# One matmul in place of two: global rows set beside the last batch's tokens in a fused sparse-attention and MLP kernel

## The chip, the cores and the metric

The kernel runs on one core of a Trainium2 chip. The metric is the device time of one execution in microseconds (us), as the median of several runs; a lower value is better. The kernel before took 382.2 us (median of 3 runs, 379.91 to 382.34). TensorE is called PE here, its weight loads PEld, VectorE DVE, ScalarE ACT, GpSimd POOL and SyncE SP, as in the profile.

## The reference: what is computed

Eight batches of 576 tokens go through eight heads of attention (head size 64). A token sees the tokens at most 32 away, and 8 global tokens, which every token sees and which see all tokens. The result, 4608 rows of 512 values, goes through a layer with 2048 inner values: `h = x @ w_in`, `g = h + sin(alpha*h)^2 / alpha`, `g @ w_out`.

```python
mask = np.abs(pos[:, None] - pos[None, :]) <= 32
mask = mask | is_global[:, None] | is_global[None, :]
scores = np.where(mask, scores, -1e9)
attn = softmax(scores)                  # rows
x = (attn @ v) as rows of 4608 x 512
h = x @ w_in                            # 512 -> 2048
s = np.sin(alpha * h)
out = (h + s * s / (alpha + 1e-9)) @ w_out
```

## The kernel before

The kernel works batch by batch. For batch b, `attention(b)` (L712) makes the normalised rows `xT`, and `gemm1(b)` (L947) makes the first product, the sine and its square, and writes the sum `g` to `H2`. `gemm2(b)` (L1028) is the second product; it is a generator, and `fill(n)` (L1069) issues its next n matmuls of 512 columns (L1033) wherever PE would have little else to do. The instructions are written in the order in which each engine takes them; each engine works through its own list in that order and waits on semaphores.

`attention` goes over four pairs of heads `hp`. For each it makes scores in three groups (L736), the exponential on ACT (L744), the mask on DVE (L747), the two products with the values and with ones (L778), an inverse of the sums on ACT (L804, L807), and on DVE two small sums over the pieces of the global rows (`sums`, L788) and the product with the inverse (`normalise`, L810). A token's row is normalised there. The 8 global rows of a batch are collected in `GS`, and after the last pair L859 takes the inverse and L860 writes them to column b of `XG`, which at the end holds 64 columns: 8 global rows times 8 batches. Besides, `beside(at)` adds small work at each pair, such as copies of the next batch's queries and keys (L347) and the squares of x (`square_x`, L892).

`gemm1` goes over 16 groups `nt` of 128 inner values. A group takes 4 steps `c` of the 512 inputs, times two halves `e` of 288 tokens: 8 matmuls (L972). Three buffers in PSUM take turns (`zn`, `zr`, `zd`), so that group nt+3 writes the buffer of group nt. The first two groups begin with steps c = 0 to 2, which need the first three pairs of heads only. After a group ACT takes the sine (L1009), ACT or DVE squares it (L1013 on ACT for nt 1, 3, 5, 8, 10, 12, 14; otherwise L1015 on DVE), and DVE makes the sum (L1020). Five matmuls of `gemm2` come after group 2, one after each of the groups 3 to 13.

In `gemm1` of the last batch (b = 7) the 64 global columns are worked too, 32 beside each half:

```python
nc.tensor.matmul(out=h[e][:, 0:HALF], lhsT=lhsT, rhs=xT[:, c, e, :], ...)         # L972
if more:
    nc.tensor.matmul(out=h[e][:, HALF:W], lhsT=lhsT,                              # L977
                     rhs=xg[:, c, e * NE : (e + 1) * NE], ...)
```

So each of 128 matmuls of 288 columns is followed by one of 32 columns with the same weights, loaded again. The sine and the square are taken over 2 x 320 columns at once, and a second, small L1020 writes the global part to `HG`.

Beside the result the kernel bounds the argument of the sine, by norms: `square_x` squares the rows and adds them up to 288 columns, `token_norms` (L903) multiplies those by ones on PE (L905) and compares on DVE (L907), and `global_norms` (L912) does the same for `XG` by a square (L916), four matmuls of 64 columns (L918) and a comparison (L920). Four of the eight `token_norms` and `global_norms` stand at the end: after the last `gemm1` come `square_x(7)`, 32 matmuls of `gemm2`, these norms, 16 more matmuls, the verdict (`judge`, L925, with one matmul, L939), the rest of `gemm2`, and the 64 global rows (`gemm2_globals`, L1051), which are written by an indirect DMA (L1061).

Of the kernel before, what the change touches and what calls it, by code (L numbers as in the profile page):

```python
# [10 lines left out]
ALU = mybir.AluOpType  # L11
AF = mybir.ActivationFunctionType
DT = mybir.dt
# [3 lines left out]
P = 128  # L17
KW = 96
NG = 8
KT = 48  # L20
# [227 lines left out]
def kernel(  # L248
# [11 lines left out]
    nc = tc.nc  # L260
# [24 lines left out]
    trp = mctx.enter_context(tc.tile_pool(name="trp", bufs=1))  # L285
    pairp = mctx.enter_context(tc.tile_pool(name="pairp", bufs=2))
    normp = mctx.enter_context(tc.tile_pool(name="normp", bufs=2))
    xpool = mctx.enter_context(tc.tile_pool(name="xpool", bufs=2))
    spool = mctx.enter_context(tc.tile_pool(name="spool", bufs=3))
    osbp = mctx.enter_context(tc.tile_pool(name="osbp", bufs=3))  # L290
    srp = mctx.enter_context(tc.tile_pool(name="srp", bufs=4))
# [19 lines left out]
    SQ = main.tile([P, CT * S], DT.bfloat16, name="SQ")  # L311
# [397 lines left out]
    xTs = {}  # L709


    def attention(b, beside):  # L712


        kx, qx, VXb = KX[b % 2], QX[b % 2], VX[b % 2]
        xT = xpool.tile([P, CT, 2, HALF], DT.bfloat16, name="xT")
        xTs[b] = xT
        GS = normp.tile([P, 2, NHP, 2, 4], DT.float32, name="GS")
        if b:
# [88 lines left out]

        def normalise(hp):
            nc.vector.tensor_tensor(  # L810
                out=xT[:, hp].rearrange("p e (k m c) -> p (e k) m c", k=2, c=KT), in0=body(hp, 0),
                in1=Rs[hp][:], op=ALU.mult,
            )

        start, per_scores = (START, PER_SCORES) if b != 1 else (0, LATE)
        def idle(hp):
            if (b == 0 and hp > 1) or (b == 1 and hp < 2):
                warm(zo[0], 1)

        fill(start)  # L820
        beside(-1)
        for hp in range(NHP):
            Es[hp] = pairp.tile([P, NT12, WCOL], DT.bfloat16, name="E")
            for g in range(2):
                scores(hp, g)
                fill(per_scores[hp][g])
                idle(hp)
            if b == 0 and hp:
                products(hp - 1, range(3), (1,))
            elif hp:  # L830
                products(hp - 1, (0, 1))
            scores(hp, 2)
# [12 lines left out]
        last = NHP - 1  # L845
# [13 lines left out]
        nc.vector.reciprocal(out=RG[:], in_=GS[:, 1])  # L859
        nc.vector.tensor_tensor(  # L860
            out=XG[:, :, :, b].rearrange("p h (c x) -> p h x c", x=2), in0=GS[:, 0], in1=RG[:], op=ALU.mult
        )
        beside(NHP)
        after.release()

# [25 lines left out]

    def square_x(b, part):  # L892

        xf = xTs[b][:].rearrange("p c e s -> p (c e s)")
        if part == 0:
            nc.vector.tensor_tensor(out=SQ[:], in0=xf, in1=xf, op=ALU.mult)
            return
        for n in (2 * S, S):
            nc.vector.tensor_tensor(out=SQ[:, 0:n], in0=SQ[:, 0:n], in1=SQ[:, n : 2 * n], op=ALU.add)
        SR[b] = srp.tile([P, HALF], DT.bfloat16, name="SR")  # L900
        nc.vector.tensor_tensor(out=SR[b][:], in0=SQ[:, 0:HALF], in1=SQ[:, HALF:S], op=ALU.add)

    def token_norms(b, pn):  # L903

        nc.tensor.matmul(out=pn[:, 0:HALF], lhsT=ones[:], rhs=SR.pop(b)[:], start=True, stop=True)  # L905
        low = normp.tile([P, HALF], DT.bfloat16, name="low")
        nc.vector.tensor_scalar(  # L907
            out=low[:], in0=pn[:, 0:HALF], scalar1=limit[:, 0:1], scalar2=0.0, op0=ALU.is_le,
            op1=ALU.add, accum_out=XC[:, b : b + 1],
        )  # L910

    def global_norms(pn):  # L912

        sg = normp.tile([P, CT, NG * B], DT.bfloat16, name="sg")
        xf = XG[:].rearrange("p c j b -> p c (j b)")
        nc.vector.tensor_tensor(out=sg[:], in0=xf, in1=xf, op=ALU.mult)  # L916
        for c in range(CT):
            nc.tensor.matmul(out=pn[:, 0 : NG * B], lhsT=ones[:], rhs=sg[:, c, :], start=c == 0, stop=c == CT - 1)  # L918
        low = normp.tile([P, NG * B], DT.bfloat16, name="lowg")
        nc.vector.tensor_scalar(  # L920
            out=low[:], in0=pn[:, 0 : NG * B], scalar1=limit[:, 0:1], scalar2=0.0, op0=ALU.is_le,
            op1=ALU.add, accum_out=XCG[:, 0:1],
        )

    def judge(pv):  # L925

        ok = [normp.tile([P, 1], DT.float32, name=f"ok{i}") for i in range(4)]
        for i, (src, lim, op) in enumerate(
            ((EA, LIM_SUM, ALU.is_le), (RA, LIM_REC, ALU.is_le), (XC, HALF - 0.5, ALU.is_ge),
             (XCG, NG * B - 0.5, ALU.is_ge))  # L930
        ):
# [15 lines left out]
    def gemm1(b):  # L947
# [1 line left out]

        xT = xTs[b]  # L950
        r0 = (b % 2) * S
        NE = NG * B // 2
        more = b == B - 1
        W = HALF + (NE if more else 0)
        xg = XG[:].rearrange("p c j b -> p c (j b)")
        hr = tc.alloc_tile_pool(name="hr", bufs=1, space=PSUM)
        hs = {}

# [2 lines left out]
        def chunks(nt, cs):  # L961
            if nt not in hs:
                if order[nt] == "o":
                    hs[nt] = [(slice(e, e + 1), zo[e][:, None, :]) for e in range(2)]
                else:
                    h = {"n": zn, "d": zd}.get(order[nt]) or hr.tile([P, 2, 512], DT.float32, name="zr")
                    hs[nt] = [(slice(0, 2), h[:])]
            h = [ap[:, i] for es, ap in hs[nt] for i in range(es.stop - es.start)]
            for c in cs:
                for e in range(2):  # L970
                    lhsT = w_in[:, c, nt * P : (nt + 1) * P]
                    nc.tensor.matmul(  # L972
                        out=h[e][:, 0:HALF], lhsT=lhsT, rhs=xT[:, c, e, :],
                        start=(c == 0), stop=(c == CT - 1), skip_group_check=True,
                    )
                    if more:
                        nc.tensor.matmul(  # L977
                            out=h[e][:, HALF:W], lhsT=lhsT, rhs=xg[:, c, e * NE : (e + 1) * NE],
                            start=False, stop=(c == CT - 1), skip_group_check=True,
                        )  # L980

        on_act = (ON_ACT_FIRST, ON_ACT_SECOND, ON_ACT)[min(b, 2)]
        for nt in range(NT):
# [29 lines left out]
                nc.scalar.activation(out=s2[:, :, 0:W], in_=sb[:, :, 0:W], func=AF.Square)  # L1013
            else:
                nc.vector.tensor_tensor(out=s2[:, :, 0:W], in0=sb[:, :, 0:W], in1=sb[:, :, 0:W], op=ALU.mult)  # L1015
            for dst, lo, hi in (
                (H2[:, nt, r0 : r0 + S], 0, HALF), (HG[:, nt, :], HALF, HALF + NE)
            )[: 1 + more]:
                for es, h in hs[nt]:
                    nc.vector.scalar_tensor_tensor(  # L1020
                        out=dst.rearrange("p (e c) -> p e c", e=2)[:, es],
                        in0=s2[:, es, lo:hi], scalar=recipT[:, nt : nt + 1], in1=h[:, :, lo:hi],
                        op0=ALU.mult, op1=ALU.add,
                    )
        hr.release()


# [168 lines left out]
```

## Time and profile before

| what | value |
|---|---|
| median of 3 runs | 382.2 us (379.91 to 382.34) |
| the profiled execution: its own time | 381.18 us |
| the profiled execution: span from first to last instruction | 379.5 us |
| granted TensorE clock, mean | 0.991 |
| busy: PE, DVE, ACT, POOL | 342.2, 288.4, 294.3, 133.8 us |
| matmuls; weight loads | 3172; 3172 |

Times are us from the start of the span. A row of the timeline has a start, a duration, the engine, the line, the operation, what it writes and reads with shapes, how often, and in brackets the idle time of the engine before it and what ended that. A group row ends in the busy time, the mean duration in ns, and the idle time before. Matmuls overlap: one takes longer from its start to its end than the distance to the next one's start, so the price of a matmul is read from the distance between starts. The same holds, less strongly, for DVE and ACT.

### The profile page before, as it was taken

What the parts mean: (1) busy time and instruction counts of PE and PEld (TensorE: products, weight loads), DVE (VectorE), ACT (ScalarE), POOL (GpSimd) and SP (SyncE); (2) the same over time, 40 slices, a digit from 0 to 9 for tenths busy, and PEclk for the clock granted to TensorE, in tenths of its full rate; (3) what the DMA queues carried; (4) which work ended last, traced back from release to release, by engine and by line L of the source; (5) the groups of instructions that cost most, each with busy time, mean ns of one, the idle gap of its engine ahead of it and who ended that gap; (6) DMA issues with size and microseconds to landing.
All of it is one profiled execution on the core that took longest, in us unless ns stands there. A gap on an engine that the chain in (4) does not pass through costs nothing. (4 is left out here: it accounts for less than half of the span.)

```text
span 379.5 us, 8635 instructions
## 1 busy us (share of the span) xinstructions
PE 342.2 (90%) x3172; PEld 233.3 (61%) x3172; DVE 288.4 (76%) x614; ACT 294.3 (78%) x566; POOL 133.8 (35%) x204
## 2 busy tenths in 40 slices
PE   2679869997998899999989999999999998999893
PEld 2567646764565666676656766666676666776341
DVE  6777897589889887988888888888788876589400
ACT  7789897898889788788878887889888888675111
POOL 7993695559477101840086006720000000000001
PEclk9999999999999999999999999999999999999998
DMA  6999999999999863789069923727111011100221
GB/s 119 119 161 186 155 153 174 147 173 179 182 181 119 137 114 74 91 99 216 28 81 94 204 62 45 75 40 155 42 44 29 0 41 46 29 3 28 57 85 48
DMA packets 103579, 38.08 MB, mean 100 GB/s; under 512 B 94138, under 2 KB 98250, under 8 KB 103082
## 3 DMA queue, kind: packets, MB, share of 16 engines
q0 software_dynamic: 56640, 18.56, 42.4%
q1 hardware_dynamic: 46890, 18.89, 25.1%
q8 instruction: 27, 0.44, 0.5%
q14 instruction: 22, 0.18, 0.1%
HBM read 37.15 MB, written 17.83 MB: 145 GB/s over the span
## 5 line engine op out<-in xcount | busy, mean ns | idle before, releaser
L1033 PE MATMUL zo<-w_out,H 128*128 128x512 bf16 x576 | 153.2, 378 | 0.0
L972 PEld LDWEIGHTS <-w_in 128*128 128x128 bf16 x1024 | 99.2, 97 | 48.4 <-issue 14.8
L390 POOL DMA_DIRECT2D VX<-in_v_dram x128 | 83.7, 663 | 105.7 <-PE zd L778 87.4
L1033 PEld LDWEIGHTS <-H 128*128 128x128 bf16 x576 | 52.0, 97 | 37.3
L744 ACT ACTIVATE E<-ring 128x480 bf16<-128x480 f32 x96 | 54.3, 568 | 24.5 <-PE ring L736 24.0
L972 PE MATMUL zn<-xT,w_in 128*128 128x288 bf16 x376 | 56.2, 285 | 4.7 <-DVE H L1020 2.0
L747 DVE TENSOR_TENSOR E<-E,MASK 128x480 bf16<-128x480 bf16 x96 | 36.6, 411 | 16.2 <-ACT E L744 15.0
L972 PE MATMUL zr<-xT,w_in 128*128 128x288 bf16 x312 | 46.7, 285 | 1.0 <-DVE H L1020 0.6
L972 PE MATMUL zd<-xT,w_in 128*128 128x288 bf16 x312 | 45.4, 285 | 1.6 <-DVE H L1020 1.5
L1020 DVE SCALAR_TENSOR_TENSOR H<-s,recipT,zn 128x576 bf16<-128x576 bf16 x47 | 38.2, 813 | 9.9 <-ACT s L1013 5.5
L1061 POOL DMA_INDIRECT out_dram<-osb,grow x1 | 1.0, 1007 | 125.8 <-SPq L1164 125.8
L1009 ACT ACTIVATE sb<-zn,alphaT 128x576 bf16<-128x576 f32 (+1 forms) x47 | 34.8, 741 | 12.6 <-PE zn L972 9.2
L1013 ACT ACTIVATE s<-sb 128x576 bf16<-128x576 bf16 (+1 forms) x62 | 42.7, 689 | 2.0
L736 PE MATMUL ring<-QX,KX 128*128 128x120 bf16 x384 | 38.3, 226 | 5.6 <-ACT E L744 2.7
L736 PEld LDWEIGHTS <-KX 128*128 128x128 bf16 x384 | 29.1, 102 | 21.7 <-issue 7.6
L1015 DVE TENSOR_TENSOR s<-sb 128x576 bf16<-128x576 bf16 (+1 forms) x66 | 31.4, 475 | 7.7 <-ACT sb L1009 7.4
L1020 DVE SCALAR_TENSOR_TENSOR H<-s,recipT,zd 128x576 bf16<-128x576 bf16 x39 | 31.7, 813 | 6.6 <-ACT s L1013 4.8
L1039 ACT COPY osb<-zo 128x512 f32<-128x512 f32 x36 | 20.8, 578 | 19.7 <-PE zo L1033 19.7
L1020 DVE SCALAR_TENSOR_TENSOR H<-s,recipT,zr 128x576 bf16<-128x576 bf16 x39 | 31.7, 813 | 4.6 <-ACT s L1013 2.5
L1009 ACT ACTIVATE sb<-zd,alphaT 128x576 bf16<-128x576 f32 (+1 forms) x39 | 28.9, 741 | 7.9 <-PE zd L972 5.3
L778 PEld LDWEIGHTS <-VX 128*128 128x128 bf16 x448 | 26.4, 99 | 12.9 <-issue 7.5
L1009 ACT ACTIVATE sb<-zr,alphaT 128x576 bf16<-128x576 f32 (+1 forms) x39 | 28.9, 741 | 4.8 <-PE zr L972 3.5
(160 smaller groups left out, 458.9 us busy)
## 6 DMA issues: line engine op xcount, KB each, us to landing
VX<-in_v_dram POOLq DMA_DIRECT2D x128, 36.0 KB, 3.6
kd<-in_k_dram POOLq DMA_DIRECT2D x7, 576.0 KB, 6.6
qd<-in_q_dram POOLq DMA_DIRECT2D x7, 576.0 KB, 8.9
w_in<-in_moe_w_in_dram POOLq DMA_DIRECT2D x4, 512.0 KB
w_out<-in_moe_w_out_dram POOLq DMA_DIRECT2D x4, 512.0 KB, 8.9
out_dram<-osb SPq DMA_DIRECT2D x8, 256.0 KB
out_dram<-osb SPq DMA_DIRECT2D x8, 224.0 KB
out_dram<-osb SPq DMA_DIRECT2D x8, 192.0 KB
```

The costliest lines, as they stand in the source:

```text
L390: nc.gpsimd.dma_start(out=VX[b % 2][r : r + 24, hp, :, t * D : t * D + D], in_=v[b, 2 * hp + t].rearrange("(i a y) d -> y a i d", a=24, y= ...
L736: nc.tensor.matmul(out=ps[:, e * WCOL : (e + 1) * WCOL], lhsT=kx[:, hp, i, :], rhs=qx[:, hp, :, s0 : s0 + 60], start=True, stop=True, skip ...
L744: nc.scalar.activation(out=Eg, in_=ps[:, 0 : 4 * WCOL], func=AF.Exp, scale=scale, accum_out=EA[:, n : n + 1])
L747: nc.vector.tensor_tensor(out=Eg, in0=Eg, in1=MASK[:, 4 * g : 4 * g + 4, :].rearrange("p i c -> p (i c)"), op=ALU.mult,)
L778: nc.tensor.matmul(out=out_t[:, half, :, a - half * CUT : z - half * CUT], lhsT=OB[:] if key else VXb[:, hp, i, :], rhs=E[:, i, :, a - s0 ...
L972: nc.tensor.matmul(out=h[e][:, 0:HALF], lhsT=lhsT, rhs=xT[:, c, e, :], start=(c == 0), stop=(c == CT - 1), skip_group_check=True,)
L1009: nc.scalar.activation(out=sb[:, es, 0:W], in_=h[:, :, 0:W], func=AF.Sin, scale=alphaT[:, nt : nt + 1])
L1013: nc.scalar.activation(out=s2[:, :, 0:W], in_=sb[:, :, 0:W], func=AF.Square)
L1015: nc.vector.tensor_tensor(out=s2[:, :, 0:W], in0=sb[:, :, 0:W], in1=sb[:, :, 0:W], op=ALU.mult)
L1020: nc.vector.scalar_tensor_tensor(out=dst.rearrange("p (e c) -> p e c", e=2)[:, es], in0=s2[:, es, lo:hi], scalar=recipT[:, nt : nt + 1], i ...
L1033: nc.tensor.matmul(out=ops[:], lhsT=H2[:, nt, blk * P : (blk + 1) * P], rhs=w_out[:, nt, :], start=(nt == 0), stop=(nt == NT - 1),)
L1039: nc.scalar.copy(out=osb[:], in_=ops[:])
```

## The change

- `XG` goes. A tile `xlast` of 4 x 2 x 320 columns takes its place and that of the x buffer of every odd batch (1, 3, 5, 7); even batches use the one buffer left in the pool. Each half has 288 token columns and then 32 global columns.
- `keep_globals` writes a batch's global rows there. It is one inverse and two products, one for each half, where L859 and L860 were one inverse and one product. In the batches 0 to 6 it stands where those stood. In batch 7 it stands twice: for the first three pairs of heads right after the `normalise` of the third, within the loop, and for the fourth pair between its `sums` and its `normalise`.
- `gemm1` has one matmul per step and half, of 288 columns, or of 320 in batch 7. The 128 matmuls of 32 columns and their weight loads go.
- `normalise` of an odd batch writes two runs of 288 that lie 320 apart; `square_x` of an odd batch reads such runs, and that of batch 7 works on 2560 columns instead of 2304.
- `token_norms` of batch 7 is one matmul of 320 columns with two comparisons; `global_norms` goes.
- The small L1020 for the global part is written separately, but is the same instruction as before.

```diff
-    xpool = mctx.enter_context(tc.tile_pool(name="xpool", bufs=2))
+    xpool = mctx.enter_context(tc.tile_pool(name="xpool", bufs=1))
...
-    XG = main.tile([P, CT, NG, B], DT.bfloat16, name="XG")
+    NE = NG * B // 2
+    xlast = main.tile([P, CT, 2, HALF + NE], DT.bfloat16, name="xlast")
...
-        xT = xpool.tile([P, CT, 2, HALF], DT.bfloat16, name="xT")
+        wide = b == B - 1
+        odd = b % 2
+        xT = xlast if odd else xpool.tile([P, CT, 2, HALF], DT.bfloat16, name="xT")
...
+        RG = normp.tile([P, NHP, 2, 4], DT.float32, name="RG")
+
+        def keep_globals(hps):
+            nc.vector.reciprocal(out=RG[:, hps], in_=GS[:, 1, hps])
+            to = xlast[:, hps, :, HALF:].rearrange("p h e (c x b) -> p h e x c b", x=2, b=B)
+            for e in range(2):
+                cs = slice(2 * e, 2 * e + 2)
+                nc.vector.tensor_tensor(
+                    out=to[:, :, e, :, :, b], in0=GS[:, 0, hps, :, cs], in1=RG[:, hps, :, cs], op=ALU.mult
+                )
...
                 normalise(hp - 1)
+                if wide and hp == last:
+                    keep_globals(slice(0, last))
...
         sums(last, 0)
+        if wide:
+            keep_globals(slice(last, NHP))
         normalise(last)
-        RG = normp.tile([P, NHP, 2, 4], DT.float32, name="RG")
-        nc.vector.reciprocal(out=RG[:], in_=GS[:, 1])
-        nc.vector.tensor_tensor(
-            out=XG[:, :, :, b].rearrange("p h (c x) -> p h x c", x=2), in0=GS[:, 0], in1=RG[:], op=ALU.mult
-        )
+        if not wide:
+            keep_globals(slice(0, NHP))
...
+        n = SR[b].shape[1]
+        nc.tensor.matmul(out=pn[:, 0:n], lhsT=ones[:], rhs=SR.pop(b)[:], start=True, stop=True)
+        for lo, hi, dst in ((0, HALF, XC[:, b : b + 1]), (HALF, n, XCG[:, 0:1])):
+            if hi > lo:
...
-        for c in range(CT):
-            nc.tensor.matmul(out=pn[:, 0 : NG * B], lhsT=ones[:], rhs=sg[:, c, :], start=c == 0, stop=c == CT - 1)
...
-                        out=h[e][:, 0:HALF], lhsT=lhsT, rhs=xT[:, c, e, :],
+                        out=h[e][:, 0:W], lhsT=lhsT, rhs=xT[:, c, e, 0:W],
                         start=(c == 0), stop=(c == CT - 1), skip_group_check=True,
                     )
-                    if more:
-                        nc.tensor.matmul(
-                            out=h[e][:, HALF:W], lhsT=lhsT, rhs=xg[:, c, e * NE : (e + 1) * NE],
-                            start=False, stop=(c == CT - 1), skip_group_check=True,
-                        )
...
-    global_norms(zd[:, 0, :])
```

More of the change, by code (lines that the diff above doesn't have):

```diff
@@ L310 @@
     tiny = main.tile([P, 1], DT.float32, name="tiny")
-    SQ = main.tile([P, CT * S], DT.bfloat16, name="SQ")
+    SQ = main.tile([P, CT * (S + NG * B)], DT.bfloat16, name="SQ")
     W2 = main.tile([P, DFF], DT.bfloat16, name="W2")
@@ L810, in normalise @@
             nc.vector.tensor_tensor(
-                out=xT[:, hp].rearrange("p e (k m c) -> p (e k) m c", k=2, c=KT), in0=body(hp, 0),
-                in1=Rs[hp][:], op=ALU.mult,
-            )
+                out=xT[:, hp, :, 0:HALF].rearrange("p e (k m c) -> p e k m c", k=2, c=KT) if odd
+                else xT[:, hp].rearrange("p e (k m c) -> p (e k) m c", k=2, c=KT),
+                in0=body(hp, 0).rearrange("p (e k) m c -> p e k m c", k=2) if odd else body(hp, 0),
+                in1=Rs[hp][:].rearrange("p (e k) m c -> p e k m c", k=2) if odd else Rs[hp][:], op=ALU.mult,
+            )
+        RG = normp.tile([P, NHP, 2, 4], DT.float32, name="RG")
[7 more added lines that the diff above has]
+                )
         start, per_scores = (START, PER_SCORES) if b != 1 else (0, LATE)
@@ L818, in idle @@
                 warm(zo[0], 1)
+        last = NHP - 1
         fill(start)
@@ L842, in attention @@
                 normalise(hp - 1)
+                if wide and hp == last:
+                    keep_globals(slice(0, last))
             fill(per_scores[hp][2])
             beside(hp)
-        last = NHP - 1
         ring.release()
@@ L892, in square_x @@
     def square_x(b, part):
-        xf = xTs[b][:].rearrange("p c e s -> p (c e s)")
+        W = HALF + (NE if b == B - 1 else 0)
+        n = 2 * CT * W
         if part == 0:
-            nc.vector.tensor_tensor(out=SQ[:], in0=xf, in1=xf, op=ALU.mult)
+            xf = xTs[b][:].rearrange("p c e s -> p (c e) s")[:, :, 0:W]
+            nc.vector.tensor_tensor(
+                out=SQ[:, 0:n].rearrange("p (g s) -> p g s", s=W), in0=xf, in1=xf, op=ALU.mult
+            )
             return
-        for n in (2 * S, S):
-            nc.vector.tensor_tensor(out=SQ[:, 0:n], in0=SQ[:, 0:n], in1=SQ[:, n : 2 * n], op=ALU.add)
@@ L900, in square_x @@
-        SR[b] = srp.tile([P, HALF], DT.bfloat16, name="SR")
-        nc.vector.tensor_tensor(out=SR[b][:], in0=SQ[:, 0:HALF], in1=SQ[:, HALF:S], op=ALU.add)
-    def token_norms(b, pn):
[L905 to L909, printed above, removed]
-        )
@@ L912, in global_norms @@
[L912 to L916, printed above, removed]
-        for c in range(CT):
[L918 to L923, printed above, removed]
+        for m in (n // 2, n // 4):
+            nc.vector.tensor_tensor(out=SQ[:, 0:m], in0=SQ[:, 0:m], in1=SQ[:, m : 2 * m], op=ALU.add)
@@ new lines, in square_x @@
+        n //= 8
+        SR[b] = srp.tile([P, n], DT.bfloat16, name="SR" if b < B - 1 else "SRl")
+        nc.vector.tensor_tensor(out=SR[b][:], in0=SQ[:, 0:n], in1=SQ[:, n : 2 * n], op=ALU.add)
+    def token_norms(b, pn):
+        n = SR[b].shape[1]
+        nc.tensor.matmul(out=pn[:, 0:n], lhsT=ones[:], rhs=SR.pop(b)[:], start=True, stop=True)
+        for lo, hi, dst in ((0, HALF, XC[:, b : b + 1]), (HALF, n, XCG[:, 0:1])):
+            if hi > lo:
+                low = normp.tile([P, hi - lo], DT.bfloat16, name="low" if hi == HALF else "lowg")
+                nc.vector.tensor_scalar(
+                    out=low[:], in0=pn[:, lo:hi], scalar1=limit[:, 0:1], scalar2=0.0, op0=ALU.is_le,
+                    op1=ALU.add, accum_out=dst,
+                )
@@ L929, in judge @@
             ((EA, LIM_SUM, ALU.is_le), (RA, LIM_REC, ALU.is_le), (XC, HALF - 0.5, ALU.is_ge),
-             (XCG, NG * B - 0.5, ALU.is_ge))
+             (XCG, NE - 0.5, ALU.is_ge))
         ):
@@ L951, in gemm1 @@
         r0 = (b % 2) * S
-        NE = NG * B // 2
         more = b == B - 1
         W = HALF + (NE if more else 0)
-        xg = XG[:].rearrange("p c j b -> p c (j b)")
         hr = tc.alloc_tile_pool(name="hr", bufs=1, space=PSUM)
@@ L972, in chunks @@
                     nc.tensor.matmul(
-                        out=h[e][:, 0:HALF], lhsT=lhsT, rhs=xT[:, c, e, :],
+                        out=h[e][:, 0:W], lhsT=lhsT, rhs=xT[:, c, e, 0:W],
                         start=(c == 0), stop=(c == CT - 1), skip_group_check=True,
                     )
-                    if more:
-                        nc.tensor.matmul(
-                            out=h[e][:, HALF:W], lhsT=lhsT, rhs=xg[:, c, e * NE : (e + 1) * NE],
-                            start=False, stop=(c == CT - 1), skip_group_check=True,
-                        )
         on_act = (ON_ACT_FIRST, ON_ACT_SECOND, ON_ACT)[min(b, 2)]
@@ L1015, in gemm1 @@
                 nc.vector.tensor_tensor(out=s2[:, :, 0:W], in0=sb[:, :, 0:W], in1=sb[:, :, 0:W], op=ALU.mult)
[L1016 to L1024, printed above, removed]
+            for es, h in hs[nt]:
+                nc.vector.scalar_tensor_tensor(
+                    out=H2[:, nt, r0 : r0 + S].rearrange("p (e c) -> p e c", e=2)[:, es],
+                    in0=s2[:, es, 0:HALF], scalar=recipT[:, nt : nt + 1], in1=h[:, :, 0:HALF],
+                    op0=ALU.mult, op1=ALU.add,
+                )
+            if more:
+                nc.vector.scalar_tensor_tensor(
+                    out=HG[:, nt, :].rearrange("p (x n) -> p x n", x=2),
+                    in0=s2[:, :, HALF:W], scalar=recipT[:, nt : nt + 1], in1=hs[nt][0][1][:, :, HALF:W],
+                    op0=ALU.mult, op1=ALU.add,
+                )
         hr.release()
```

## The prediction

> **What bounds the kernel now.** I read the page's busy shares first, then the busy time by stretch for the end of the program (the change's large edits lie there), then the timeline of PE and DVE there, the waits, and the built program's order of instructions and semaphores. The chain that ended last reaches back 1.3 us only and says nothing here.
>
> ```profile
> PE 342.2 (90%) x3172; PEld 233.3 (61%) x3172; DVE 288.4 (76%) x614; ACT 294.3 (78%) x566; POOL 133.8 (35%) x204
> 321.19:345.81 24.62, 23.04 (x276) 17.26 (x274) 18.48 (x40) 17.94 (x26) 0.00 (x0) 1.00 0.04 12
> 345.81:352.71 6.90, 6.90 (x35) 3.13 (x33) 5.46 (x11) 2.25 (x4) 0.00 (x0) 1.00 0.26 76
> 352.71:355.27 2.56, 1.09 (x9) 0.50 (x8) 2.07 (x9) 0.00 (x0) 0.00 (x0) 1.00 0.00 0
> ```
>
> A stretch's row has its length, then the busy time of PE, PEld, DVE, ACT and POOL, the granted clock and the DMA share. PE is the busiest engine in the whole, and nearly always busy in the last gemm1 (321.19 to 345.81) and in the 32 matmuls behind it; the clock is full. In the norms (352.71 to 355.27) PE is busy for 1.09 of 2.56 us: a chain between PE and DVE is the bound there. After that come matmuls of gemm2 to the end. So a microsecond that PE gains before 355.27 is a microsecond of the whole, if nothing else becomes late.
>
> **The price of a pair of matmuls.** Distances between starts:
>
> ```profile
> 287.64 1.14 PE L972 MATMUL zr<-xT,w_in 128*128 128x288 bf16 x8
> 288.62 0.38 PE L1033 MATMUL zo<-w_out,H 128*128 128x512 bf16 x1
> ...
> 328.96 0.28 PE L972 MATMUL zr<-xT,w_in 128*128 128x288 bf16 x1
> ...
> 330.14 0.38 PE L1033 MATMUL zo<-w_out,H 128*128 128x512 bf16 x1
> ...
> 345.81 7.07 PE L1033 MATMUL zo<-w_out,H 128*128 128x512 bf16 x32
> ```
>
> Eight matmuls of 288 columns in batch 6 take 288.62 - 287.64 = 0.98 us, 122.5 ns each. Eight pairs (288 and 32) in batch 7 take 330.14 - 328.96 = 1.18 us, 147.5 ns each. So 32 columns alone cost 25 ns. The 32 matmuls of 512 from 345.81 to 352.71 cost 215.6 ns each. The slope between 288 and 512 is 93.1 / 224 = 0.416 ns a column, so 320 columns cost 122.5 + 13.3 = 135.8 ns. Its bounds are the 122.5 of the narrower matmul and the 147.5 of the pair; I take 135.8, on the line between the two nearest widths. Saved: 128 x 11.7 = 1.5 us of PE.
>
> Here a rule speaks for much more: the Trainium skill, "TensorE: Matmul & The Clock Gate", section "Back-to-back issue gap", gives about 81 ns for N=128 and 131 ns for N=512 in a stream of loads and matmuls, by which 32 columns would be some 69 ns and the pair's merger worth about 65 ns, 8.3 us in all. The trace disagrees: 122.5 and 25 ns above, where that page would have 102 and 69. The rows decide.
>
> **The start of the last gemm1.**
>
> ```profile
> 319.13 0.23 DVE L788 TENSOR_REDUCE GS<-zd 128x8 f32<-128x64 f32 x1 [0.22 <-ACT L L804]
> 319.27 0.21 DVE L788 TENSOR_REDUCE GS<-zn 128x8 f32<-128x64 f32 x1
> ...
> 319.94 0.76 DVE L810 TENSOR_TENSOR xT<-zn,R 128x576 bf16<-128x576 f32 x1 [0.45 <-ACT R L807]
> ...
> 321.39 0.23 DVE L788 TENSOR_REDUCE GS<-zd 128x8 f32<-128x64 f32 x1 [0.49 <-PE zd L778]
> 321.54 0.75 DVE L810 TENSOR_TENSOR xT<-zd,R 128x576 bf16<-128x576 f32 x1
> 322.20 0.34 DVE L859 RECIPROCAL RG<-GS 128x32 f32<-128x32 f32 x1
> 322.58 0.29 DVE L860 TENSOR_TENSOR XG<-GS,RG 128x32 bf16<-128x32 f32 x1
> ...
> 321.19 0.29 PE L972 MATMUL zn<-xT,w_in 128*128 128x288 bf16 x1
> 322.92 0.18 PE L977 MATMUL zn<-XG,w_in 128*128 128x32 bf16 x1 [1.44 <-DVE XG L860]
> ```
>
> PE issues one matmul at 321.19 and then stands until 322.92: its second matmul reads XG, and XG comes last on DVE (322.58 + 0.29, and 0.05 to reach PE). After the change, the built program shows the first matmul waiting for the first product of the early `keep_globals`, the second for its second product, and only step c = 3 for the last `normalise`. The early `keep_globals` starts behind the third `normalise`, at 319.94 + 0.66 (distance 321.54 to 322.20) = 320.60; its inverse 0.38, its products at 320.98 and 321.1 (two independent small operations start 0.14 apart, 319.13 to 319.27), so PE starts at about 321.3 and 321.45. Twelve matmuls at 135.8 ns fill until 322.9. The late `keep_globals`: sum at 321.39, inverse at 321.66 (0.23 and some 0.04), products at 322.0 and 322.1, `normalise` at 322.2, its end at 322.95, PE at 323.0. So c = 3 can start at 323.0, with 12 matmuls done; before, PE had one pair's first half done at 322.92. Without other waits gemm1 then ends at 323.0 + 116 x 0.1358 + 16 x 0.2156 = 342.2, against 345.81.
>
> Here a rule speaks against the change: the Trainium skill, "VectorE: DVE Perf Modes", section "The DRAIN you can't avoid", lets the next operation start only once the pipe is empty, by which a second product would cost its whole 0.29 us. The rows show 0.14 for two such operations of 0.23. By the page c = 3 would start 0.15 us later and the other batches would pay double below.
>
> **What is late next.** A PSUM buffer's round, on a group whose square is on ACT:
>
> ```profile
> 341.76 0.38 PE L1033 MATMUL zo<-w_out,H 128*128 128x512 bf16 x1
> 341.95 0.80 ACT L1009 ACTIVATE sb<-zn,alphaT 128x640 bf16<-128x640 f32 x1 [0.55 <-PE zn L977]
> 342.78 0.74 ACT L1013 ACTIVATE s<-sb 128x640 bf16<-128x640 bf16 x1
> 343.55 0.81 DVE L1020 SCALAR_TENSOR_TENSOR H<-s,recipT,zn 128x576 bf16<-128x576 bf16 x1 [0.29 <-ACT s L1013]
> 344.28 0.27 DVE L1020 SCALAR_TENSOR_TENSOR HG<-s,recipT,zn 128x64 bf16<-128x64 bf16 x1
> 344.47 0.49 DVE L1015 TENSOR_TENSOR s<-sb 128x640 bf16<-128x640 bf16 x1
> 345.06 0.82 DVE L1020 SCALAR_TENSOR_TENSOR H<-s,recipT,zr 128x576 bf16<-128x576 bf16 x1
> ```
>
> From the group's last matmul (its fill starts at 341.76) to the buffer's release: 344.28 + 0.27 + 0.05 - 341.76 = 2.84 us. Meanwhile PE has three fills and two groups: 0.647 + 2 x 1.18 = 3.01 us before, 0.647 + 2 x 1.086 = 2.82 after. The slack of 0.17 us goes, and each late step of ACT or DVE becomes a wait of PE. DVE needs 0.73 + 0.19 = 0.92 us for a group, and 0.59 more where it squares (344.47 to 345.06): 1.51, against 1.30 of PE; two such follow each other at nt 6 and 7, and at 15 behind 14. I stepped the 16 groups through with these distances, each starting at the later of PE's own time and the buffer's release: before, this gives 0.3 us of waits, where the trace has 345.81 less 128 x 0.1475, 16 x 0.2156 and the start at 322.80 (one distance ahead of 322.92) = 0.7; after, it gives 1.0. With the 0.4 that the stepping misses, 1.4 us of waits, and the end at 342.2 + 1.4 = 343.6. **Gain by then: 2.2 us** (3.6 if nothing is late; about 0.7 less than 2.2 if the waits double).
>
> **The norms at the end.**
>
> ```profile
> 348.78 1.35 DVE L896 TENSOR_TENSOR SQ<-xT 128x2304 bf16<-128x2304 bf16 x1
> ...
> 351.45 0.31 DVE L901 TENSOR_TENSOR SR<-SQ 128x288 bf16<-128x288 bf16 x1
> 352.71 0.29 PE L905 MATMUL zn<-SR,ones 128*128 128x288 bf16 x1
> ...
> 354.05 0.28 PE L905 MATMUL zd<-SR,ones 128*128 128x288 bf16 x1 [0.15 <-DVE low L907]
> ...
> 355.16 0.28 PE L918 MATMUL zd<-sg,ones 128*128 128x64 bf16 x4 [0.82 <-DVE sg L916]
> 355.27 0.38 PE L1033 MATMUL zo<-w_out,H 128*128 128x512 bf16 x1
> ```
>
> The four L918 wait 0.82 us for a square that stands behind all L907. Without them gemm2 goes on right after the fourth L905: 354.05 + 0.136 in place of 355.27. **Gain 1.1 us.** The wider `square_x(7)` (2560 for 2304) takes a ninth more of 351.76 - 348.78 = 2.98 us, at most 0.33: SR is ready 0.6 us ahead of L905 instead of 0.95, if DVE and PE move alike. So it costs nothing here; if DVE is 0.6 us later than PE, it costs the rest. The added comparison of 32 columns replaces one of 64, and the verdict's matmul waits for 16 matmuls anyway.
>
> **The other batches.** DVE makes two products for one at the end of each attention.
>
> ```profile
> 163.70 0.29 DVE L860 TENSOR_TENSOR XG<-GS,RG 128x32 bf16<-128x32 f32 x1
> 164.00 0.93 DVE L347 COPY QX<-qt 64x1152 bf16<-64x1152 bf16 x2
> 165.00 0.46 DVE L1015 TENSOR_TENSOR s<-sb 128x576 bf16<-128x576 bf16 x1
> ...
> 126.03 1.14 PE L972 MATMUL zn<-xT,w_in 128*128 128x288 bf16 x8 [1.12 <-DVE H L1020]
> ...
> 207.10 1.14 PE L972 MATMUL zn<-xT,w_in 128*128 128x288 bf16 x8 [0.31 <-DVE H L1020]
> ...
> 286.45 1.14 PE L972 MATMUL zn<-xT,w_in 128*128 128x288 bf16 x8 [0.23 <-DVE H L1020]
> ```
>
> DVE goes from L860 through the copies to the first square without a gap, and PE's group 3 waits for the sum behind it in the batches shown. So here the second product is not hidden: 0.14 us each, in four or five batches. **Loss 0.6 us** (bounds 0 and, at 0.29 each, 1.5). The broken rows of xlast I cost at nothing: `normalise` already reads runs of 48 from PSUM, and the square reads few, long runs. The bound from above is the rival below; the bound from below is 0. The xlast tile adds no wait on another engine in the built program; ACT, POOL and SP keep their lists as they were.
>
> **Sum.** -2.2 - 1.1 + 0.6 = -2.7 us: span 379.5 to 376.8, the profiled execution's 381.18 to 378.5. That execution stood 1.0 below the median of 382.2; the predicted median is 382.2 - 2.7 = 379.5 us, 0.7% faster. A measurement of this kernel can tell about 1% (3.8 us) from no change, so this counts as within 1%.
>
> **Rivals.** *Nothing is late next*: gemm1 gains the full 3.6 and the other batches lose 0.2: -4.5, 377.7 us. For it: ACT and DVE are busy 18 of 24.6 us; against it: the slack of 0.17 in the round. *DVE takes the gain*: the stall goes but DVE paces gemm1(7), its lag reaches L905 through `square_x`, and only the norms' 1.1 less 0.6 is left: -0.5, 381.7. For it: 1.51 against 1.30 where DVE squares; against: 0.92 where it doesn't. *Weight loads set the pace*: if the 128 loads that go free so much of PE that DVE alone bounds the last gemm1, DVE has 16 x 0.92 + 9 x 0.59 = 20.0 us of work from about 324.3 (323.0, a matmul and a sine of 0.8) and ends at 344.3 instead of 348.78: -4.4 - 1.1 + 0.6, 377.3; the 25 ns of a short matmul with its load speak against it. The Trainium skill's spacing quoted above would lead here. *The broken tiles cost time* (the other side): if an output in two runs halves `normalise`, each of 16 in the odd batches takes 0.66 us more, and PE waits for `normalise` each time: 10.6 - 2.7, 390 us. It decides from (3.8 + 2.7) / 16 = 0.41 us each; 48-element runs at full pace speak against it.
>
> **How the numbers follow.** The forecast 0.58, nothing late 0.21, DVE takes it 0.12, weight loads 0.03, broken tiles 0.06. Range 377.3 to 382.0: it takes in the second, third and fourth with the unknown bounds, and leaves out the broken tiles. Faster by over 1% (under 378.4): both gaining rivals and a tenth of the forecast, 0.29; slower by over 1%: 0.06; within: 0.65.
>
> **What would show it.** In the changed profile: no stall of PE at the first matmuls of the last gemm1 and c = 3 at about 1.8 us after the first; 8 matmuls of 320 in 1.09 us; new waits on L1020 between them, 1.0 to 1.8 us in sum; the norms' stretch 1.5 us long; the two products 0.14 apart; `normalise` of odd batches at 0.76. A `normalise` or square that is longer in odd batches, or a stretch of gemm1(7) that isn't near 22 us, would make me wrong.

## The result and the profile after

The changed kernel takes 378.22 us (median of 9 runs, 376.68 to 379.82), the kernel before 381.25 us beside it (9 runs): a ratio of 0.9921, 95% interval 0.9896 to 0.9945. That is 3.0 us less, 0.8%, where 2.7 us and 0.7% were forecast. Two later measurements of the same kernel gave 0.9904 (0.9873 to 0.9935) and 0.9897 (0.9873 to 0.9920). The comparisons use undisturbed executions alone.

The profiled execution took 376.68 us, with a span of 375.0, which is 4.5 us below the span shown before. Not all of that is the change. Where the time went is read from the busy time by stretch of the kernel after. The columns are as above, with GB/s moved by DMA as the last; the first row runs from the start of gemm1 of batch 3 to that of batch 7, then come the last gemm1, the 32 matmuls, the norms, the matmuls up to the global rows, and the rest.

```profile
160.81:319.64 158.83, 154.70 (x1413) 107.24 (x1435) 130.32 (x261) 133.18 (x262) 34.12 (x52) 1.00 0.46 77
319.64:341.57 21.93, 21.66 (x145) 13.29 (x145) 18.37 (x42) 17.72 (x26) 0.00 (x0) 1.00 0.04 13
341.57:348.48 6.91, 6.86 (x33) 3.14 (x32) 5.82 (x11) 2.33 (x4) 0.00 (x0) 1.00 0.26 76
348.48:349.96 1.48, 0.83 (x6) 0.39 (x5) 1.16 (x5) 0.00 (x0) 0.00 (x0) 1.00 0.00 0
349.96:364.32 14.36, 14.26 (x67) 6.38 (x67) 2.52 (x18) 2.34 (x4) 0.00 (x0) 1.00 0.27 75
364.32:375.00 10.68, 3.64 (x17) 1.68 (x16) 0.00 (x0) 1.17 (x2) 1.00 (x1) 0.86 0.14 43
```

And the stretches of the kernel before that were not shown:

```profile
162.31:321.19 158.88, 156.01 (x1436) 107.25 (x1434) 129.85 (x254) 133.15 (x262) 34.43 (x52) 1.00 0.46 77
355.27:369.63 14.36, 14.36 (x71) 6.39 (x69) 1.91 (x14) 2.35 (x4) 0.00 (x0) 1.00 0.28 75
369.63:379.50 9.87, 3.65 (x17) 1.68 (x16) 0.00 (x0) 1.17 (x2) 1.01 (x1) 0.83 0.16 46
```

From gemm1 of batch 3 to that of batch 7 the two are equal (158.83 and 158.88). The last gemm1 went from 24.62 to 21.93 us, the norms from 2.56 to 1.48; the stretches between and behind them are equal. The end, with the last copy and the indirect DMA, is 0.8 us longer, and everything ahead of gemm1 of batch 3 is 1.5 us shorter (it starts at 160.81 instead of 162.31). Neither can be put down to the change: over the twelve profiles taken, of the two kernels and the variants below, that start lies between 160.8 and 163.5 us, and three profiles of this same kernel have 160.81, 162.25 and 161.11; the end varies from 9.5 to 10.7 us. What the change does by the stages of the two profiles is -2.7 - 1.1 = -3.8 us, which is inside the intervals above.

The start of the last gemm1, on DVE and PE, in the timeline of the kernel after (here `sums` is L791, `normalise` L813, `keep_globals` L823 and L827, the matmul of `gemm1` L982, of `gemm2` L1041, of the norms L928):

```profile
318.37 0.76 DVE L813 TENSOR_TENSOR xlast<-zn,R 128x576 bf16<-128x576 f32 x1 [0.45 <-ACT R L810]
319.04 0.29 DVE L823 RECIPROCAL RG<-GS 128x24 f32<-128x24 f32 x1
319.37 0.29 DVE L827 TENSOR_TENSOR xlast<-GS,RG 128x12 bf16<-128x12 f32 x2
319.54 0.22 DVE L791 TENSOR_REDUCE GS<-zr 128x8 f32<-128x64 f32 x1
319.82 0.22 DVE L791 TENSOR_REDUCE GS<-zd 128x8 f32<-128x64 f32 x1
319.96 0.19 DVE L823 RECIPROCAL RG<-GS 128x8 f32<-128x8 f32 x1
320.19 0.25 DVE L827 TENSOR_TENSOR xlast<-GS,RG 128x4 bf16<-128x4 f32 x2
320.34 0.75 DVE L813 TENSOR_TENSOR xlast<-zd,R 128x576 bf16<-128x576 f32 x1
...
318.99 0.79 PE L781 MATMUL zd<-E,VX 128*128 128x88 bf16 x14
319.64 0.97 PE L982 MATMUL zn<-xlast,w_in 128*128 128x320 bf16 x6
320.45 0.98 PE L982 MATMUL zr<-xlast,w_in 128*128 128x320 bf16 x6
321.26 0.43 PE L982 MATMUL zn<-xlast,w_in 128*128 128x320 bf16 x2
```

No row of PE carries a wait. The early products start at 319.37, behind the third `normalise`, and both end by 319.66. PE works on the products with the values (L781) until it issues the first matmul at 319.64, so the first early product, 0.09 us ahead of the second, is ready only just in time. Twelve matmuls run to 321.26, and by then the last `normalise` (320.34 + 0.75) is done too. The stall of 1.44 us is gone. `normalise` (L813) takes 0.76 and 0.75 us with its two runs, as before.

Later in the same stage, and in the norms:

```profile
329.28 0.38 PE L1041 MATMUL zo<-w_out,H 128*128 128x512 bf16 x1
329.69 1.26 PE L982 MATMUL zr<-xlast,w_in 128*128 128x320 bf16 x8
330.79 0.38 PE L1041 MATMUL zo<-w_out,H 128*128 128x512 bf16 x1
...
329.36 0.28 DVE L1028 SCALAR_TENSOR_TENSOR HG<-s,recipT,zr 128x64 bf16<-128x64 bf16 x1
...
348.48 0.29 PE L928 MATMUL zn<-SR,ones 128*128 128x288 bf16 x1
349.82 0.30 PE L928 MATMUL zd<-SRl,ones 128*128 128x320 bf16 x1 [0.16 <-DVE low L932]
349.96 3.61 PE L1041 MATMUL zo<-w_out,H 128*128 128x512 bf16 x15
```

Eight matmuls of 320 columns take 330.79 - 329.69 = 1.10 us, 137 ns each (forecast 135.8). Ahead of the group at 329.69 PE is free at 329.28 + 0.216 = 329.50 and waits 0.19 us: the small sum (L1028) of the group three before, in the same buffer `zr`, ends at 329.36 + 0.28 = 329.64, and 0.05 us later PE starts. This is the buffer's round of the prediction. Such gaps between groups are 0.9 to 1.0 us in all (21.93 less 128 x 0.1367 and 16 x 0.2156 is 0.98, with the rounding of the distances). In the norms the next matmul of gemm2 comes 0.14 us after the fourth of L928.

### The profile page after: what moved, and what is told of

The parts are those of the page before. It is cut to its first block, busy times and chain, and to the rows that moved or that the text cites. A ratio compares the mean times of both kernels' runs of the same rounds, so it can differ in the third digit from the quotient of the medians.

```text
span 375.0 us, 8335 instructions
## 1 busy us (share of the span) xinstructions
PE 337.6 (90%) x2994; PEld 228.9 (61%) x3040; DVE 287.8 (77%) x624; ACT 294.1 (78%) x566; POOL 132.1 (35%) x204
## 5 line engine op out<-in xcount | busy, mean ns | idle before, releaser
L1041 PE MATMUL zo<-w_out,H 128*128 128x512 bf16 x530 | 143.3, 379 | 1.9
L982 PEld LDWEIGHTS <-w_in 128*128 128x128 bf16 x1024 | 98.6, 98 | 48.0 <-issue 12.6
L1041 PEld LDWEIGHTS <-H 128*128 128x128 bf16 x576 | 52.2, 97 | 37.9 <-issue 0.3
L1020 DVE TENSOR_TENSOR s<-sb 128x576 bf16<-128x576 bf16 (+1 forms) x66 | 31.1, 472 | 5.7 <-ACT sb L1014 5.4
L781 PEld LDWEIGHTS <-VX 128*128 128x128 bf16 x448 | 26.0, 98 | 12.5 <-issue 6.8
L982 PE MATMUL zn<-xlast,w_in 128*128 128x288 bf16 (+1 forms) x192 | 28.8, 289 | 1.2 <-DVE H L1022 0.7
L781 PE MATMUL zn<-E,VX 128*128 128x120 bf16 (+2 forms) x336 | 26.3, 209 | 3.7 <-DVE xlast L813 2.2
L982 PE MATMUL zn<-xT,w_in 128*128 128x288 bf16 x184 | 26.9, 286 | 3.0 <-DVE H L1022 1.9
```

The lines of the kernel that those rows point to most:

```text
L781: nc.tensor.matmul(out=out_t[:, half, :, a - half * CUT : z - half * CUT], lhsT=OB[:] if key else VXb[:, hp, i, :], rhs=E[:, i, :, a - s0 ...
L982: nc.tensor.matmul(out=h[e][:, 0:W], lhsT=lhsT, rhs=xT[:, c, e, 0:W], start=(c == 0), stop=(c == CT - 1), skip_group_check=True,)
L1041: nc.tensor.matmul(out=ops[:], lhsT=H2[:, nt, blk * P : (blk + 1) * P], rhs=w_out[:, nt, :], start=(nt == 0), stop=(nt == NT - 1),)
```

## The experiments

Each kernel below is the kernel after with an edit. The main reading is a stretch of the profile, from the start of gemm1 of batch 6 to the first matmul of the norms: it is 68.05, 68.02 and 68.02 us in three profiles of the kernel after, and 70.68 in the one of the kernel before. The kernel before, then the kernel after:

```profile
282.03:352.71 70.68, 68.86 (x666) 47.20 (x664) 53.88 (x109) 53.74 (x94) 0.00 (x0) 1.00 0.10 31
280.43:348.48 68.05, 67.08 (x529) 43.25 (x536) 54.38 (x114) 53.62 (x94) 0.00 (x0) 1.00 0.10 32
```

Whole times were measured in five rounds beside the kernel before, and tell about 1 us apart.

**One matmul made two again.**

```diff
-    nc.tensor.matmul(out=h[e][:, 0:W], lhsT=lhsT, rhs=xT[:, c, e, 0:W], ...)
+    nc.tensor.matmul(out=h[e][:, 0:HALF], lhsT=lhsT, rhs=xT[:, c, e, 0:HALF], ...)
+    if more:
+        nc.tensor.matmul(out=h[e][:, HALF:W], lhsT=lhsT, rhs=xT[:, c, e, HALF:W], start=False, ...)
```

> The changed kernel with one part undone: the matmul of 320 columns in batch 7 is again one of 288 and one of 32, both from xlast. Theory of the forecast (a PE price of 25 ns for the short matmul, partly hidden by waits for a PSUM buffer that come back shorter): gemm1 of batch 7 grows from 21.93 us by 0.7 us (the stepping through the groups with 147.5 ns a pair), and its waits on the sum shrink from 0.9 to about 0.2. If nothing hides, it grows by 128 x 10.8 ns = 1.4 us. If weight loads set the pace (the spacing of some 65 ns for the short matmul), it grows by several us. The whole follows: 0.7 us over the changed kernel, 2.3 us under the kernel before.

```profile
281.51:350.24 68.73, 68.48 (x667) 47.29 (x664) 54.39 (x114) 53.63 (x94) 0.00 (x0) 1.00 0.10 32
```

The stretch is 68.73 us, 0.7 more than the kernel after, as the stepping through the groups had it. A pair costs only 10.8 ns more than the wide matmul (147.5 to 136.7), and half of 128 x 10.8 ns = 1.4 us is hidden by waits that PE has anyway. Weight loads do not set the pace, or several us would have come back. The whole, 377.64 us with a ratio of 0.9920 (0.9897 to 0.9942), does not resolve 0.7 us.

**The global rows once, after the last `normalise`.**

```diff
-                if wide and hp == last:
-                    keep_globals(slice(0, last))
...
-        if wide:
-            keep_globals(slice(last, NHP))
         normalise(last)
-        if not wide:
-            keep_globals(slice(0, NHP))
+        keep_globals(slice(0, NHP))
```

> The changed kernel with one part undone: in batch 7 the global rows are written once, after the last normalise. Theory: the first matmul of gemm1 waits for both products, 321.4 instead of 319.64 on the changed kernel's clock, nothing covers that wait, and the stretch of gemm1 grows by 1.6 to 1.8 us. Rival (ACT and DVE pace the stage, so that its start matters less): under 0.8 us.

```profile
322.00 0.97 PE L977 MATMUL zn<-xlast,w_in 128*128 128x320 bf16 x6 [1.50 <-DVE xlast L827]
```

```profile
281.16:350.82 69.66, 67.75 (x538) 43.29 (x536) 54.21 (x111) 53.58 (x94) 0.00 (x0) 1.00 0.10 31
```

The stall is back, 1.50 us on the products (L827), and the stretch is 69.66, 1.64 us more. The whole: 379.01 us, ratio 0.9944 (0.9918 to 0.9970). So the largest single part of the gain is the early writing of the first three pairs' global rows, not the merging of the matmuls.

**The norms of the global rows apart.**

```diff
-        W = HALF + (NE if b == B - 1 else 0)
+        W = HALF
...
         token_norms(b, (zn, zd)[n % 2][:, 0, :])
+    global_norms(zd[:, 0, :])
```

> The changed kernel with one part undone: the norms of the global rows are a square, four matmuls of 64 and a comparison of their own again. Theory: the stretch from the first matmul of the norms to the next matmul of gemm2 is 2.56 us again instead of 1.48, and the whole is 1.1 us slower than the changed kernel. Rival (the matmuls behind it catch up, or the end is set elsewhere): the stretch grows but the distance from it to the end shrinks, and the whole stays.

```profile
281.81:349.82 68.01, 67.59 (x538) 43.23 (x536) 54.14 (x114) 53.62 (x94) 0.00 (x0) 1.00 0.11 32
349.82:352.38 2.56, 1.09 (x9) 0.50 (x8) 2.07 (x9) 0.00 (x0) 0.00 (x0) 1.00 0.00 0
```

The first stretch is as in the kernel after, the norms take 2.56 us again, and from there to the global rows it is 14.37 us, where the kernel after has 14.36, so nothing is caught up. 1.08 us, as forecast. The whole: 378.4 us, ratio 0.9937 (0.9918 to 0.9956).

**All three undone, the layout left.** The three edits together.

> All three undone at once: of the change only xlast, its two runs, and the second small product are left. Theory: the three terms are all there is, and the whole is that of the kernel before, or 0.1 to 0.2 us more (five batches, 0.03 us each); gemm1 of batch 7 takes 24.6 us and the norms 2.56. Rival (the layout did something by itself in the first batches, where the changed kernel's profile is 2.1 us shorter by the start of gemm1 of batch 2): 1 to 2 us under the kernel before.

```profile
281.35:351.61 70.26, 68.62 (x666) 47.29 (x664) 53.99 (x111) 53.62 (x94) 0.00 (x0) 1.00 0.10 31
351.61:354.17 2.56, 1.09 (x9) 0.49 (x8) 2.07 (x9) 0.00 (x0) 0.00 (x0) 1.00 0.00 0
```

The whole is that of the kernel before: 380.49 us, ratio 1.0001 (0.9983 to 1.0020). So the layout by itself does nothing that these runs can tell (within 0.8 us either way). gemm1 of batch 3, which the expectation calls batch 2, starts at 161.75, within the spread given above. The three parts taken singly (0.7, 1.6, 1.1) sum to 3.4 us; all three together are 70.26 + 2.56 - 68.02 - 1.48 = 3.3. The stretch is 0.4 us shorter than that of the kernel before, and the last gemm1 takes 24.2 us where 24.6 were expected. In the kernel before DVE waited once in that stage for its own square:

```profile
335.19 0.81 DVE L1020 SCALAR_TENSOR_TENSOR H<-s,recipT,zn 128x576 bf16<-128x576 bf16 x1 [0.46 <-DVE s L1015]
```

None of the other eleven profiles has such a wait. The group of PE that needs this buffer, group 9, starts 15.06 us behind the first matmul of the stage there, and 14.69 us in the kernel with the three edits undone: 0.37 of the 0.4 us lie at this place. What made DVE wait is not shown, nor whether it does so in every execution, since the kernel before was profiled once.

**Ten small products instead of two, in the batches 0 to 6.**

```diff
-            for e in range(2):
+            for e in range(2) if b == B - 1 else 5 * (0, 1):
```

> The changed kernel with ten small products instead of two in each of the batches 0 to 6 (the same values written five times over). Theory of the forecast (the chain from these products through the copies to the first sum is open, and PE waits at group 3): eight more at 0.10 us each put 0.8 us on group 3 of the batches 2 to 6, 3 to 4 us in all, over the changed kernel. Rival (the chain is covered, and the small loss in the changed kernel is for that reason): under 1 us.

```profile
206.13 1.38 DVE L827 TENSOR_TENSOR xlast<-GS,RG 128x16 bf16<-128x16 f32 x10
...
207.53 1.05 DVE L348 COPY QX<-qt 64x1152 bf16<-64x1152 bf16 x2
...
210.03 1.14 PE L982 MATMUL zn<-xT,w_in 128*128 128x288 bf16 x8 [1.10 <-DVE H L1022]
```

The whole is 384.3 us, ratio 1.0108 (1.0078 to 1.0138), some 7 us over the kernel after, where 3 to 4 were expected. The chain is open, as forecast: group 3 of batch 4 waits 1.10 us, but the size was not foreseen. The step from ten products to the copies (207.53 - 206.13 = 1.40 us) is not eight times 0.10 more than with two. The products write the same places five times over, and each pair waits for the pair before it (pairs start 0.26 us apart, the two of a pair 0.09), so 1.07 us came on top instead of 0.8. In the kernel after the same step is:

```profile
162.19 0.32 DVE L827 TENSOR_TENSOR xlast<-GS,RG 128x16 bf16<-128x16 f32 x2
...
162.52 1.09 DVE L348 COPY QX<-qt 64x1152 bf16<-64x1152 bf16 x2
```

0.33 us for two products of 16 elements, where the kernel before had 0.30 for one of 32. The second product costs 0.03 us net, not 0.14. Two of the five batches lost more than 1.1 us here (some 2.5 each). For batch 2 the last section shows why. In batch 5 DVE came so late that its copies and its first square ran beside copies of POOL into `KX`:

```profile
248.76 2.06 DVE L348 COPY QX<-qt 64x1152 bf16<-64x1152 bf16 x2
250.85 0.98 DVE L1020 TENSOR_TENSOR s<-sb 128x576 bf16<-128x576 bf16 x1
...
249.63 1.89 POOL L369 COPY KX<-kTg 64x384 bf16<-64x384 bf16 x2
...
252.80 1.14 PE L982 MATMUL zn<-xlast,w_in 128*128 128x288 bf16 x8 [2.64 <-DVE H L1022]
```

In the kernel after the same copies take 0.92 us and the square 0.46. Over the twelve profiles, from 110 us on, this square takes 0.45 to 0.46 us with no copy of POOL beside it (528 times) and 0.83 to 1.00 us with one beside it (12 times).

**Matmuls of gemm2 in the gaps.** Four more between the groups of the last gemm1 and six between the norms, taken from the end.

```diff
+    PER_LAST = (0, 0, 6, 1, 1, 1, 2, 1, 1, 2, 1, 1, 1, 2, 0, 0)
...
-            fill((GROUP_LATE if b == 1 else PER_GROUP)[nt])
+            fill((GROUP_LATE if b == 1 else PER_LAST if more else PER_GROUP)[nt])
...
         token_norms(b, (zn, zd)[n % 2][:, 0, :])
+        fill((0, 4, 2, 0)[n])
```

> A version that may beat both: four more matmuls of gemm2 between the groups of the last gemm1 (after the groups 2, 6, 9 and 13, where PE waits for a buffer), and six between the norms of the end; the same number fewer at the very end. Theory (PE's waits there are for a buffer's round and for DVE's comparisons, and a matmul of 216 ns fits into them): gemm1 of batch 7 stays within 0.2 us of 21.93 though it holds four more, the norms' stretch takes some 1.7 us and holds six more, so the whole is 1.7 us under the changed kernel. Rival (the round isn't what PE waits for; the fills only push the groups back): 0.9 us less gain, from the norms alone.

The first measurement was too wide: 376.83 us (373.65 to 383.43), ratio 0.9870 (0.9829 to 0.9911), beside 377.0 for the kernel after, which was run again there:

> The changed kernel once more, on this chip: a second profile and a second measure. Theory: the first two batches differ between executions through their loads, so that the start of gemm1 of batch 2 lies between 160.5 and 162.5 us in any kernel; the last gemm1 takes 21.9 us and the norms 1.48 in every profile. 3.0 us under the kernel before, 2.1 to 4.0. Rival: the first batches are shorter by the change itself, so that gemm1 of batch 2 starts at 160.8 in every profile of the changed layout.

It gave 0.9904, and its profile 68.02 us for the stretch and 1.48 for the norms; its gemm1 of batch 3 (the expectation calls it batch 2) starts at 162.25, so the rival on the first batches falls. The range of 160.5 to 162.5 us was too narrow as well: in the version with fills above it starts at 163.52. Why it varies is not shown. The version with fills was then run again, with one that takes eight more fills in earlier batches, and the kernel after a third time:

```diff
             fill((GROUP_LATE if b == 1 else PER_LAST if more else PER_GROUP)[nt])
+            fill({2: 5, 4: 1, 5: 1, 6: 1}.get(b, 0) if nt == 2 else 0)
```

> The version with fills in the last gemm1 and the norms once more, since its single runs spread from 373.65 to 383.43. Theory: 1.85 us under the changed kernel on the same chip, as its profile has it from the start of gemm1 of batch 6 to the global rows (82.02 against 83.87 us). Rival: the profile's gain doesn't show in the whole, under 0.8 us.

> The version with fills in the last gemm1 and the norms, and eight more matmuls of gemm2 taken from the end: five more after group 2 of batch 2, one more after group 2 of the batches 4, 5 and 6, where PE waits 1.16, 0.3, 0.24 and 0.25 us for the sum in the changed kernel. Theory (the chain from the small products to that sum is open, so PE has idle time that a fill can take): 1.5 us under the version without them, 3.3 under the changed kernel, 6.4 us (1.7%) under the kernel before. Rival (the fills delay ACT and DVE, or the copies of gemm2's results, and the wait returns elsewhere): no gain over that version.

> The changed kernel a third time, beside the two versions with fills: 2.1 to 4.0 us under the kernel before, and 83.9 us from the start of gemm1 of batch 6 to the global rows.

The version with fills, and after it the one with more of them (there the first row runs from gemm1 of batch 2 to that of batch 6; it is 161.82 in the kernel after):

```profile
280.71:348.75 68.04, 67.78 (x543) 43.68 (x541) 54.51 (x114) 53.87 (x95) 0.00 (x0) 1.00 0.10 32
348.75:350.54 1.79, 1.79 (x11) 0.97 (x10) 1.33 (x5) 0.35 (x1) 0.00 (x0) 1.00 0.14 33
```

```profile
119.78:281.62 161.84, 158.09 (x1459) 108.22 (x1456) 136.19 (x271) 134.09 (x263) 48.66 (x74) 1.00 0.60 95
```

The stretch holds four more matmuls in the same 68.04 us, and the norms hold six more in 1.79 us, in which PE is busy throughout. So PE's waits there, for a buffer's round and for the comparisons, could be filled. Whole times on one chip: 377.03 us for the kernel after (ratio 0.9897, 0.9873 to 0.9920), 375.34 with fills (0.9852, 0.9825 to 0.9879), 374.21 with more fills (0.9819, 0.9791 to 0.9847). Fills brought 1.7 us where 1.85 were expected, and more fills 1.1 us on top where 1.5 were; the intervals of these two versions overlap, so the whole times alone don't tell them apart. In the last version seven more matmuls stand in the batches 2 to 5 at no cost (161.84 and 161.82): the open chain behind the small products shows as idle time of PE there. But from gemm1 of batch 6, which holds the eighth, to the norms it takes 0.35 us more than the version with fills (68.39 and 68.04):

```profile
281.62:350.01 68.39, 67.99 (x544) 43.87 (x542) 54.36 (x113) 53.90 (x95) 0.00 (x0) 1.00 0.09 29
```

```profile
330.95 0.59 ACT L1048 COPY osb<-zo 128x512 f32<-128x512 f32 x1
```

In the last gemm1 ACT makes a copy of gemm2's results here, ahead of a sine, and group 9 comes 0.35 us later than in the version with fills. There ACT makes two such copies in that stage, at 324.16 and 339.55, clear of this place. So a part of the rival came true: the copies that belong to the fills fell elsewhere. This version still beats both kernels: 6.6 us under the kernel before.

## Why the prediction was right, point by point

- *The price of a pair.* 135.8 ns was forecast for 320 columns, 137 measured; 128 x 11.7 ns = 1.5 us of PE was right within a tenth. It is worth only 0.7 us in the stretch, which undoing it alone showed.
- *The start.* No stall, and step c = 3 at 1.62 us behind the first matmul instead of 1.8. That is twelve matmuls and no wait: the inverse over 8 elements took 0.19 us where the row for 32 has 0.34, so the last `normalise` ended at 321.09, ahead of PE, and the early products came just as PE needed them. Worth 1.6 us, the largest part.
- *What is late next.* Right in kind: 0.9 to 1.0 us of waits between the groups. 1.4 had been put in: 1.0 by stepping and 0.4 that the stepping missed in the kernel before. That 0.4 came back neither in the three profiles of the kernel after nor with the old order in the new layout. It lies at the single wait of DVE for its own square, and it should not have been carried over. The gain of 2.2 us was forecast; 2.7 by the two profiles, and 2.25 against the kernel with the three edits undone.
- *The norms.* 1.1 forecast, 1.08 measured; `square_x` with its ninth more is done in time.
- *The other batches.* The step that was mis-sized: 0.6 us of loss was forecast, and none is seen (201.06 us from gemm1 of batch 2 to that of batch 7 in the kernel before; 201.11, 201.00 and 201.01 in three profiles of the kernel after). The chain is as open as it was said to be, as ten products and the free fills show; but the second product costs 0.03 us net instead of 0.14, since each product is half as wide (0.23 us instead of 0.29), and two without a wait between them start 0.09 apart.
- *The broken rows of xlast* cost nothing: `normalise` at 0.75 and 0.76 us, and with all else undone the ratio is 1.0001 (0.9983 to 1.0020).
- *The rivals.* "Nothing is late next" falls by the gaps that fills could use. "DVE takes the gain" falls by the 2.7 us. "Weight loads set the pace" falls by the 0.7 us of the split, and by a last gemm1 that gained 2.7 us and not 4.4. "The broken tiles cost time" falls by the layout alone.

The sum came out at -2.7 where the stages of the two profiles have -3.8: the loss that wasn't there (0.6) and the wait that doesn't come back (0.4) both stood on the side of caution. The whole times say -3.0, -3.7 and -3.9 in three measurements, so that the first came within 0.3 us of the forecast is in part luck.

## What to carry to other kernels

Merging a narrow matmul into its neighbour saves its issue time, here 11 ns of 147, and part of that returns as waits of the chain behind it; what gated the first matmul, a small operation written last, was worth more than 128 merged matmuls. So look first at what the first instruction of a stage waits for, and whether part of it can be written earlier. Where a stage runs at a buffer's round and other work is pending, place that work in the gaps: four matmuls of 216 ns in gaps of some 0.2 us were free. But look where the work that hangs on them falls: one copy that landed ahead of a sine cost 0.35 us.

## What the hardware showed that was not expected

In the kernel with ten products, group 3 of batch 2 waited 2.09 us, and behind that wait PE ran at half its clock. The timeline:

```profile
125.43 1.98 PE L982 MATMUL zn<-xT,w_in 128*128 128x288 bf16 x8 [2.09 <-DVE H L1022]
127.21 0.63 PE L1041 MATMUL zo<-w_out,H 128*128 128x512 bf16 x1
127.64 1.81 PE L982 MATMUL zr<-xT,w_in 128*128 128x288 bf16 x8
```

Eight matmuls took 1.98 and 1.81 us instead of 1.14: the granted clock was 0.50 from 125.56 to 128.97. Half the clock for 3.41 us costs about 1.7 us, on top of the wait. The Trainium skill, "TensorE: Matmul & The Clock Gate", section "HAM oscillation — how this bites in real kernels", warns of gaps over about 3.4 us; here one of 2.09 us was enough.

The length of a wait does not decide by itself. In the same kernel group 3 of batch 5 waited 2.64 us, and the clock stayed at 1.00. In the kernel before a wait of 1.75 us at 52.39 stands ahead of half the clock from 55.23 to 58.64; in the second profile of the kernel after a wait of 1.74 us at 53.27 left it at 1.00.

The twelve profiles show a grid. Counted from the point where the clock first rose, it fell and rose again only at whole multiples of 3.41 us. Cut by this grid, the 2.09 us lie in one piece, in which PE is busy for 1.27 us, and the 2.64 us are split between two pieces, in which it is busy for 1.67 and 2.46 (the granted clock is third from the right):

```profile
122.15:125.56 3.41, 1.27 (x7) 0.54 (x7) 3.23 (x9) 1.64 (x3) 0.52 (x1) 1.00 1.17 180
125.56:128.97 3.41, 3.41 (x15) 2.07 (x14) 1.75 (x4) 1.42 (x2) 0.00 (x0) 0.50 0.89 186
248.44:251.85 3.41, 1.67 (x10) 0.87 (x9) 3.33 (x6) 2.28 (x4) 3.29 (x5) 1.00 0.93 119
251.85:255.26 3.41, 2.46 (x19) 1.83 (x19) 2.72 (x4) 1.25 (x2) 0.53 (x2) 1.00 0.14 23
```

Over the twelve profiles, without their last 12 us, half the clock followed each of the nine pieces in which PE was busy for less than 1.5 us, one of two pieces with 1.54 and 1.60 us, and no piece with more. So a wait of some 2 us can cost nearly twice its length, if most of it falls into one piece of the grid; no run here moved a wait on purpose to test this.
